# Decode attention with a token mixer: blocks of 16384 keys instead of 8192, 64 KB rows for V, and a new order of the loads at both ends

## The chip, the core and the metric

The kernel runs on one core of one Trainium2 chip. The metric is the device time of one execution in microseconds; the profile adds one execution taken by the hardware profiler.

## What is computed

One token `x` of 448 numbers goes through two branches, and a gate mixes them (bf16 inputs; the caches hold 65536 keys for each of 8 key heads, two query heads share one key head):

```python
g = sigmoid((x * gate_w).sum())                       # one number
q = (x @ wq).reshape(16 heads, 256)                   # wq: 448 x 4096
scores = q . k_cache * 256 ** -0.5                    # k_cache: 8 x 65536 x 256
o = softmax(scores) @ v_cache                         # v_cache: 8 x 65536 x 256
a = o.reshape(4096) @ wo                              # wo: 4096 x 448
h = layernorm(x)
b = gelu(outer(h, w1) + b1) @ w2 + b2                 # the mixer, 448 x 1792
out = g * a + (1 - g) * b
```

The two caches are 537 MB in all, read once.

## The kernel before

The work goes through 64 blocks of `BLK` = 8192 keys, eight for each key head. A block's K and V are each one load of 4 MB, in which a partition gets 64 consecutive keys, a row of 32 KB. There are two tiles for K and two for V, used in turn (`k_tiles`, `v_tiles`, 32 KB per partition each).

Every instruction that is recorded through `seq` is held to its order in the program on its own engine, so the order below is the order on each queue. All large loads stand on one queue, that of SyncE (SP). A load waits there until its tile is free, and whatever stands behind it on SP waits too. Besides, each load takes one of eight completion semaphores in turn, and waits until the load that held it before has landed.

Opening. SP loads `wq` (L109, three rows of 8 KB together on each partition, and the last 64 rows of the matrix in two loads, L112) into what is later a V tile. The queue of ScalarE (ACT) loads `x` three ways: copied to all partitions (`xb`, L115), as columns (`xm`, L117) and its last 64 numbers twice (`xt`, L119); then the mixer's small vectors and `gate_w` (L122 to L126). SP goes on with block 0's K in four pieces and block 1's K (L144, L145, issued at L132). TensorE forms the query with 128 matmuls (L194, L201), VectorE (DVE) the layernorm (L223 to L240), ScalarE fourteen gelu rows (`gel`, L245) into the other V tile. DVE then copies the query into `qpad` and computes `gate` (L267) from an exponential that stands on ScalarE behind the gelu rows (L256).

A block. `transposes` turns four groups of 128 keys on TensorE into a PSUM tile, one of three `tps`, and DVE copies it to `kT` (L316, L321). `scores` multiplies with the query (L331); it stands some groups behind the transposes. A block has 16 such groups of four. After the last scores of block `n` the program issues the load of V(n) and of K(n+2), takes the maximum of each row (L356), and does the product with V of the block before, `pv` (64 matmuls of 256 columns, L346), around the rest of the softmax. So `pv` runs one block behind the scores:

```python
        load_v(n, WHOLE if n < NBLK - 1 else LAST)
        if n + 2 < NBLK:
            load_k(n + 2, WHOLE)
        max_rows(n)
        if n > 0:
            pv(n - 1, 0, 32)
        max_heads(n)
        if n > 0:
            pv(n - 1, 32, KP)
        softmax(n)
```

In block 0 the load of `wo` (L462) and the mixer's product (`mixer_tail`, L280) stand between the scores and the load of V. When a key head is done, `denominators`, `head_out` and `project` carry its result through `wo` into `a_acc`, inside the next block's groups.

End. The V of the last block comes in five pieces (`LAST`: 2 MB, 1 MB, 512 KB and twice 256 KB). After the last piece come its `pv`, the accumulation (L400), `head_out` (L420), `project` (L433), two additions (L486, L487) and the store (L490).

Of the kernel before, what the change touches and what calls it, by code (L numbers as in the profile page):

```python
# [8 lines left out]
FP32 = mybir.dt.float32  # L9
# [10 lines left out]


BLK = 8192
KP = BLK // 128


NJ = 16
NI = KP // NJ
ROWS = REP * NI


@with_exitstack
def kernel(
# [26 lines left out]

    last = {}  # L60

    def seq(ins):
# [19 lines left out]
    v_tiles = [kvpool.tile([128, KP, DH], BF16, name=f"vt{i}") for i in range(2)]  # L82
    kT_tiles = [work.tile([128, NJ, 128, 2], BF16, name=f"kT{i}") for i in range(2)]
    p_tiles = [work.tile([128, 512], BF16, name=f"p_sb{i}") for i in range(2)]
    pT_tiles = [work.tile([128, 512], BF16, name=f"pT{i}") for i in range(2)]
    wo_sb = const.tile([128, HQ, 2, D], BF16)

    tps = [psum.tile([128, 512], FP32, name=f"tps{i}") for i in range(3)]
    sc_ps = [psum.tile([128, 512], FP32, name=f"sc_ps{i}") for i in range(2)]
    pv_ps = psum.tile([128, DH], FP32, name="pv_ps")  # L90
# [4 lines left out]
    xm = const.tile([128, 3], BF16)  # L95
    xt = const.tile([128, 1], BF16)
    xb = const.tile([128, D], BF16)
# [6 lines left out]
    wq_m = v_tiles[1][:, 0:48, :].rearrange("p a b -> p (a b)").rearrange(  # L104
        "p (k n) -> p k n", k=3
    )
    wq_t = v_tiles[1][:, 48:56, :].rearrange("p a b -> p (a b)")

    seq(nc.sync.dma_start(out=wq_m, in_=A_wq[0:DM, :].rearrange("(p k) n -> p k n", k=3)))  # L109
    DT = D - DM  # L110
    for h in range(2):
        seq(nc.sync.dma_start(  # L112
            out=wq_t[DT * h:DT * (h + 1), :], in_=A_wq[DM:D, 2048 * h:2048 * (h + 1)]
        ))
    seq(nc.scalar.dma_start(out=xb[:], in_=A_x[0, 0].partition_broadcast(128)))  # L115
    with nc.allow_non_contiguous_dma(reason="short rows"):
        seq(nc.scalar.dma_start(out=xm[:], in_=A_x[0, 0, 0:DM].rearrange("(p k) -> p k", k=3)))  # L117
        for h in range(2):
            seq(nc.scalar.dma_start(  # L119
                out=xt[DT * h:DT * (h + 1), :], in_=A_x[0, 0, DM:D].rearrange("(r o) -> r o", o=1)  # L120
            ))
        seq(nc.scalar.dma_start(out=w1b[:], in_=B_w1[0].rearrange("(p b) -> p b", b=NF)))  # L122
        seq(nc.scalar.dma_start(out=b1b[:], in_=B_b1.rearrange("(p b) -> p b", b=NF)))
        seq(nc.scalar.dma_start(out=w2b[:], in_=B_w2.rearrange("(p b) o -> p (b o)", b=NF)))
        seq(nc.scalar.dma_start(out=gw[:], in_=gate_w.rearrange("(o n) -> o n", o=1)))
        seq(nc.scalar.dma_start(out=b2b[:], in_=B_b2.rearrange("(o n) -> o n", o=1)))  # L126

    def load_k(n, pieces):
        g, b = divmod(n, NB)
        src = A_k_cache[0, g, b * BLK:(b + 1) * BLK, :].rearrange("(p j) d -> p j d", j=KP)  # L130
        for j0, j1 in pieces:
            seq(nc.sync.dma_start(out=k_tiles[n % 2][:, j0:j1, :], in_=src[:, j0:j1, :]))  # L132

    def load_v(n, pieces):
        g, b = divmod(n, NB)
        src = A_v_cache[0, g, b * BLK:(b + 1) * BLK, :].rearrange("(p j) d -> p j d", j=KP)
        for j0, j1 in pieces:
            seq(nc.sync.dma_start(out=v_tiles[n % 2][:, j0:j1, :], in_=src[:, j0:j1, :]))

    WHOLE = [(0, KP)]  # L140
    QUARTERS = [(i * NJ, (i + 1) * NJ) for i in range(NI)]
    LAST = [(0, 32), (32, 48), (48, 56), (56, 60), (60, 64)]

    load_k(0, QUARTERS)  # L144
    load_k(1, WHOLE)  # L145


# [4 lines left out]


    val = const.tile([128, REP], FP32)
    seq(nc.vector.tensor_reduce(
        out=val[:],
        in_=ident_f[:].rearrange("p (a i r) -> p r a i", a=4, r=REP)[:, :, :, 0:NI],
        op=ALU.add, axis=AXIS.XY,
    ))
    fst = const.tile([128, REP], FP32)  # L160
    seq(nc.vector.tensor_reduce(
        out=fst[:],
        in_=ident_f[:].rearrange("p (a i r) -> p r a i", a=4, r=REP)[:, :, :, 0:1],
        op=ALU.add, axis=AXIS.XY,
# [5 lines left out]
    ones_row = const.tile([1, 128], FP32)  # L170
    seq(nc.vector.memset(ones_row[:], 1.0))

# [9 lines left out]
    xtm = const.tile([128, 2], BF16)  # L182
    seq(nc.vector.memset(xtm[:], 0.0))
    for h in range(2):
        seq(nc.vector.tensor_copy(
            out=xtm[DT * h:DT * (h + 1), h:h + 1], in_=xt[DT * h:DT * (h + 1), :]
        ))
    q_ps = hd_ps[:, 0:2 * HQ]
    for h in range(HQ):
        half, hh = divmod(h, HQ // 2)  # L190
        for c in range(2):
            col = c * HQ + h
            for k in range(3):
                seq(nc.tensor.matmul(  # L194
                    q_ps[:, col:col + 1],
                    lhsT=wq_m[:, k, h * DH:(h + 1) * DH].rearrange("p (d c) -> p c d", c=2)[:, c, :],
                    rhs=xm[:, k:k + 1],
                    start=(k == 0),
                    stop=False,
                ))  # L200
            seq(nc.tensor.matmul(  # L201
                q_ps[:, col:col + 1],
                lhsT=wq_t[:, hh * DH:(hh + 1) * DH].rearrange("p (d c) -> p c d", c=2)[:, c, :],
                rhs=xtm[:, half:half + 1],
                start=False,
                stop=True,
            ))
# [12 lines left out]
    gel = v_tiles[0][:].rearrange("p a b -> p (a b)")[:, 0:NF * D].rearrange(  # L220
        "p (b n) -> p b n", b=NF
    )
    seq(nc.vector.tensor_copy(out=xf[:], in_=xb[:]))  # L223
# [25 lines left out]

# [8 lines left out]

    seq(nc.vector.tensor_copy(
# [14 lines left out]

# [18 lines left out]
    acc = work.tile([128, DH], FP32)  # L293
# [6 lines left out]
    den_tiles = [work.tile([128, 1], FP32, name=f"den{i}") for i in range(2)]  # L300
    al_tiles = [work.tile([128, 1], FP32, name=f"al{i}") for i in range(3)]
    rden = work.tile([128, 1], FP32)
    esc = work.tile([128, REP], FP32)
    oT = work.tile([128, 2, REP], BF16)
    a_acc = const.tile([1, D], FP32)
    res = const.tile([1, D], BF16)

    state = {"t": 0}

    def transposes(n, i, quarter):  # L310

        kT = kT_tiles[(n * NI + i) % 2]
        tp = tps[state["t"] % 3]
        state["t"] += 1
        for jj in range(4):
            seq(nc.tensor.transpose(  # L316
                tp[:, jj * 128:(jj + 1) * 128],
                k_tiles[n % 2][:, i * NJ + quarter * 4 + jj, :].bitcast(FP32),
                ident_f[:, :],
            ))  # L320
        seq(nc.vector.tensor_copy(  # L321
            out=kT[:, quarter * 4:(quarter + 1) * 4, :, :].rearrange("p j n c -> p (j n c)"),
# [3 lines left out]
    def scores(n, i, c):  # L326
        kT = kT_tiles[(n * NI + i) % 2]
        S = sc_ps[n % 2]
        g = n // NB
        for a in range(4):  # L330
            seq(nc.tensor.matmul(  # L331
                S[32 * a:32 * (a + 1), :],
                lhsT=qpad[:, c, g, i, :],
                rhs=kT[:, :, 32 * a:32 * (a + 1), c],
# [5 lines left out]
    def pv(n, j0, j1):  # L340
        pT = pT_tiles[n % 2]
        vt = v_tiles[n % 2]
        for j in range(j0, j1):
            i, jj = divmod(j, NJ)
            grp = j % 4
            seq(nc.tensor.matmul(  # L346
                pv_ps[32 * grp:32 * grp + REP, :],
                lhsT=pT[:, 32 * jj + REP * i:32 * jj + REP * (i + 1)],
                rhs=vt[:, j, :],
                start=(j < 4),  # L350
                stop=(j >= KP - 4),
# [3 lines left out]
    def max_rows(n):  # L355
        seq(nc.vector.tensor_reduce(  # L356
            out=rmax[:], in_=sc_ps[n % 2][:, :], op=ALU.max, axis=AXIS.X
        ))
        seq(nc.tensor.transpose(sm_ps[0:1, 0:128], rmax[:, 0:1], ident_f[:, :]))  # L359

    def max_heads(n):
        b = n % NB
# [5 lines left out]
        if b > 0:  # L368
            seq(nc.vector.tensor_tensor(out=mrun[:], in0=mrun[:], in1=mnew[:], op=ALU.max))
        seq(nc.tensor.matmul(  # L370
            sm_ps[:, 128:128 + REP], lhsT=ones_row[0:1, :], rhs=mrun[0:1, :], start=True, stop=True
        ))

    def softmax(n):
        b = n % NB
        nb, nb_old = nb_tiles[n % 2], nb_tiles[(n + 1) % 2]
        den, al = den_tiles[n % 2], al_tiles[n % 3]
        seq(nc.vector.tensor_tensor_reduce(  # L378
            out=junk[:], in0=sm_ps[:, 128:128 + REP], in1=nval[:], scale=1.0, scalar=0.0,
            op0=ALU.mult, op1=ALU.add, accum_out=nb[:, 0:1],  # L380
        ))
        if b > 0:
# [3 lines left out]
        seq(nc.scalar.activation(  # L386
            out=p_tiles[n % 2][:, :], in_=sc_ps[n % 2][:, :], func=ACT.Exp, scale=scale,
            bias=nb[:, 0:1], accum_out=den[:, 0:1],
        ))
        seq(nc.vector.transpose(out=pT_tiles[n % 2][:, :], in_=p_tiles[n % 2][:, :]))  # L390
# [7 lines left out]
    def accumulate(n):  # L398
        if n % NB > 0:
            seq(nc.vector.scalar_tensor_tensor(  # L400
                out=acc[:], in0=acc[:], scalar=al_tiles[n % 3][:, 0:1], in1=pv_ps[:, :],
                op0=ALU.mult, op1=ALU.add,
            ))
        else:
            seq(nc.vector.tensor_copy(out=acc[:], in_=pv_ps[:, :]))
# [11 lines left out]
    def head_out():  # L417

        for c in range(2):
            seq(nc.tensor.matmul(  # L420
                hd_ps[:, 464 + REP * c:464 + REP * (c + 1)],
                lhsT=acc[:].rearrange("p (d c) -> p c d", c=2)[:, c, :], rhs=esc[:],
                start=True, stop=True,
            ))
        seq(nc.vector.tensor_copy(
            out=oT[:], in_=hd_ps[:, 464:464 + 2 * REP].rearrange("p (c r) -> p c r", c=2)
        ))

    def project(g):
        a_ps = hd_ps[0:1, 0:D]  # L430
        for r in range(REP):
            for c in range(2):
# [3 lines left out]
                ))  # L436
        if g == 0:
# [83 lines left out]
```

## Time and profile before

| what | value |
|---|---|
| median of 3 runs | 1296.43 us (1296.35 to 1297.05) |
| the profiled execution's own time | 1297.59 us |
| its span, first to last instruction | 1295.8 us |
| busy share: TensorE matmul, weight load, VectorE, ScalarE | 76%, 54%, 64%, 6% |
| mean granted TensorE clock | 0.904 |
| read from HBM | 544.34 MB, 420 GB/s over the span |
| loads of 4 MB: K, V | 63, 63; 27.3 and 32.2 us from issue to landing (median) |

The profile gives busy time in microseconds for each engine, a rate and a share for the 16 DMA engines, and for each group of instructions its count, its mean duration and what ended the idle time before it. A share over the whole span is a mean over stages; the stages here are the opening (about 50 us), the blocks, and the end (about 30 us). A load's time from issue to landing includes the time it is queued behind other loads.

### The profile page before, as it was taken

How to read it: one execution, taken by the hardware profiler on the slowest of the kernel's cores; microseconds unless marked ns; L12 is line 12 of the kernel's file. 1: busy time of each engine (PE TensorE's matmuls, PEld its weight loads, DVE VectorE, ACT ScalarE, POOL GpSimd, SP SyncE). 2: the span in 40 equal slices, each digit the busy share in tenths (PEclk: the TensorE clock that was granted, in tenths of full speed). 3: DMA queues.
4: the chain of work that ended last, by engine and by line, in shares of the span. 5: the costliest groups of instructions: out<-in, count | busy, mean ns of one | idle time of the engine just before them, and what ended most of it. 6: DMA issues, size and time to landing. Idle time of an engine off the chain costs nothing.

```text
span 1295.8 us, 24075 instructions
## 1 busy us (share of the span) xinstructions
PE 983.7 (76%) x10654; PEld 705.8 (54%) x10654; DVE 823.9 (64%) x1599; ACT 73.5 (6%) x203; POOL 2.4 (0%) x7
## 2 busy tenths in 40 slices
PE   3877877877877877778878778778778687777786
PEld 2554655555654655555655555546556456555554
DVE  3665766756766666666657657567566566666664
ACT  4000000000000000000000000000000000000000
POOL 0000000000000000000000000000000000000000
PEclk9988989988989889889889889898898898889898
DMA  8999999999999999999999999999999999999995
GB/s 333 412 430 429 432 430 426 434 426 432 431 426 432 429 430 431 427 433 432 427 432 429 430 430 429 432 426 432 432 424 434 427 430 432 426 421 425 429 429 218
DMA packets 22798, 545.88 MB, mean 421 GB/s; under 512 B 2980, under 2 KB 5158, under 8 KB 5670
## 3 DMA queue, kind: packets, MB, share of 16 engines
q1 hardware_dynamic: 21810, 544.22, 98.2%
q8 instruction: 83, 1.36, 0.4%
q10 hardware_dynamic: 884, 0.13, 0.1%
q14 instruction: 21, 0.17, 0.0%
HBM read 544.34 MB, written 0.00 MB: 420 GB/s over the span
## 4 chain that ended last, share of the span: by engine, by line
DMA 66%; PE 31%; DVE 1%; ACT 1%; issue 0%; ACTq 0%; SPq 0%; DVEq 0%
DMA kn<-in_A_k_cache_dram 64%; PE tps L316 24%; PE sc_ps L331 5%; DMA vt<-in_A_v_cache_dram 2%; DMA xt<-in_A_x_dram 1%; ACT vt L245 1%; PE hd_ps L433 1%; PE pv_ps L346 0%; PE hd_ps L420 0%; DVE kT L321 0%; PE hd_ps L280 0%; DVE rmax L356 0%; ACT L256 0%; PE sm_ps L370 0%; PE sm_ps L359 0%
## 5 line engine op out<-in xcount | busy, mean ns | idle before, releaser
L321 DVE COPY kT<-tps 128x1024 bf16<-128x1024 bf16 x1024 | 655.6, 685 | 231.8 <-PE tps L316 229.3
L316 PE MATMUL tps<-ident_f,kn 128*128 128x128 f32 x4096 | 642.2, 309 | 177.3 <-DMA kn<-in_A_k_cache_dram 172.2
L316 PEld LDWEIGHTS tps<-ident_f,kn 128*128 128x128 f32 x4096 | 522.9, 158 | 294.3 <-DMA kn<-in_A_k_cache_dram 189.7
L331 PE MATMUL sc_ps<-kT,qpad 128*32 128x512 bf16 x2048 | 195.4, 392 | 50.0 <-DVE kT L321 49.2
L346 PE MATMUL pv_ps<-vt,pT 128*2 128x256 bf16 x4096 | 148.4, 291 | 1.3 <-DMA vt<-in_A_v_cache_dram 1.2
L331 PEld LDWEIGHTS <-qpad 128*32 128x32 bf16 x2048 | 52.9, 93 | 126.8 <-issue 117.2
L346 PEld LDWEIGHTS <-pT 128*2 128x2 bf16 x4096 | 90.1, 87 | 28.0 <-issue 2.4
L390 DVE STREAM_TRANSPOSE pT<-p_sb 128x512 bf16<-128x512 bf16 x64 | 45.5, 711 | 64.8 <-ACT p_sb L386 64.8
L383 ACT ACTIVATE al<-nb,nb 128x1 f32<-128x1 f32 x56 | 16.5, 295 | 1038.5 <-DVE nb L378 1038.5
L356 DVE TENSOR_REDUCE rmax<-sc_ps 128x1 f32<-128x512 f32 x64 | 44.2, 691 | 45.5 <-PE sc_ps L331 45.5
L359 PE MATMUL sm_ps<-ident_f,rmax 128*1 128x128 f32 x64 | 17.3, 270 | 52.4 <-DVE rmax L356 52.4
L378 DVE CUSTOM_DVE_ANT_0 junk<-sm_ps,nval 128x2 f32<-128x2 f32 x64 | 10.2, 159 | 68.9 <-PE sm_ps L370 68.9
L386 ACT ACTIVATE p_sb<-sc_ps,nb 128x512 bf16<-128x512 f32 x64 | 42.9, 670 | 156.7 <-DVE nb L378 156.7
L359 PEld LDWEIGHTS sm_ps<-ident_f,rmax 128*1 128x1 f32 x64 | 5.1, 79 | 84.4 <-DVE rmax L356 84.4
L370 PEld LDWEIGHTS sm_ps<-mrun,ones_row 1*128 1x128 f32 x128 | 20.8, 202 | 16.7 <-issue 16.2
L400 DVE SCALAR_TENSOR_TENSOR acc<-acc,al,pv_ps 128x256 f32<-128x256 f32 x56 | 26.5, 472 | 4.0 <-PE pv_ps L346 4.0
L370 PE MATMUL sm_ps<-mrun,ones_row 1*128 1x2 f32 x128 | 26.3, 272 | 0.3 <-DVE mrun L363 0.3
L363 DVE TENSOR_REDUCE mnew<-sm_ps 1x2 f32<-1x32 f32 x56 | 10.0, 178 | 20.3 <-PE sm_ps L359 20.3
L194 PE MATMUL hd_ps<-xm,vt 128*128 128x1 bf16 x96 | 3.6, 165 | 12.4 <-DMA xm<-in_A_x_dram 12.4
L386 ACT ACTIVATION_READ_ACCUMULATOR p_sb<-sc_ps,nb 128x1 f32 x64 | 12.2, 191 | 0.0
L194 PEld LDWEIGHTS <-vt 128*128 128x128 bf16 x96 | 3.6, 104 | 12.3 <-DMA vt<-in_A_wq_dram 12.1
L392 DVE SCALAR_TENSOR_TENSOR lsum<-lsum,al,den 128x1 f32<-128x1 f32 x56 | 9.9, 177 | 0.0
(66 smaller groups left out, 94.2 us busy)
## 6 DMA issues: line engine op xcount, KB each, us to landing
kn<-in_A_k_cache_dram SPq DMA_DIRECT2D x63, 4096.0 KB, 27.3
vt<-in_A_v_cache_dram SPq DMA_DIRECT2D x63, 4096.0 KB, 32.2
kn<-in_A_k_cache_dram SPq DMA_DIRECT2D x4, 1024.0 KB, 11.1
wo_sb<-in_A_wo_dram SPq DMA_DIRECT2D x1, 3584.0 KB
vt<-in_A_wq_dram SPq DMA_DIRECT2D x1, 3072.0 KB
vt<-in_A_v_cache_dram SPq DMA_DIRECT2D x1, 2048.0 KB, 19.7
vt<-in_A_v_cache_dram SPq DMA_DIRECT2D x1, 1024.0 KB
vt<-in_A_wq_dram SPq DMA_DIRECT2D x2, 256.0 KB, 4.1
```

The lines of the kernel that those rows point to most:

```text
L245: seq(nc.scalar.activation(out=gel[:, b, :], in_=h_bc[:], func=ACT.Gelu_apprx_tanh, scale=w1f[:, b:b + 1], bias=b1f[:, b:b + 1],))
L316: seq(nc.tensor.transpose(tp[:, jj * 128:(jj + 1) * 128], k_tiles[n % 2][:, i * NJ + quarter * 4 + jj, :].bitcast(FP32), ident_f[:, :],))
L321: seq(nc.vector.tensor_copy(out=kT[:, quarter * 4:(quarter + 1) * 4, :, :].rearrange("p j n c -> p (j n c)"), in_=tp[:, :].bitcast(BF16),))
L331: seq(nc.tensor.matmul(S[32 * a:32 * (a + 1), :], lhsT=qpad[:, c, g, i, :], rhs=kT[:, :, 32 * a:32 * (a + 1), c], start=(i == 0 and c == 0 ...
L346: seq(nc.tensor.matmul(pv_ps[32 * grp:32 * grp + REP, :], lhsT=pT[:, 32 * jj + REP * i:32 * jj + REP * (i + 1)], rhs=vt[:, j, :], start=(j ...
L356: seq(nc.vector.tensor_reduce(out=rmax[:], in_=sc_ps[n % 2][:, :], op=ALU.max, axis=AXIS.X))
L359: seq(nc.tensor.transpose(sm_ps[0:1, 0:128], rmax[:, 0:1], ident_f[:, :]))
L370: seq(nc.tensor.matmul(sm_ps[:, 128:128 + REP], lhsT=ones_row[0:1, :], rhs=mrun[0:1, :], start=True, stop=True))
L383: seq(nc.scalar.activation(out=al[:], in_=nb_old[:], func=ACT.Exp, scale=-1.0, bias=nb[:, 0:1]))
L386: seq(nc.scalar.activation(out=p_tiles[n % 2][:, :], in_=sc_ps[n % 2][:, :], func=ACT.Exp, scale=scale, bias=nb[:, 0:1], accum_out=den[:, ...
L390: seq(nc.vector.transpose(out=pT_tiles[n % 2][:, :], in_=p_tiles[n % 2][:, :]))
L400: seq(nc.vector.scalar_tensor_tensor(out=acc[:], in0=acc[:], scalar=al_tiles[n % 3][:, 0:1], in1=pv_ps[:, :], op0=ALU.mult, op1=ALU.add,))
```

## The change

A block now has 16384 keys, so there are 32 blocks, four for each key head. On a partition a block has 128 consecutive keys, 64 KB in each cache.

- V has one tile, `vt`, of 64 KB per partition, and one load of 8 MB per block. K keeps two tiles; they are the two halves of one block, each a load of 4 MB with 32 KB from every 64 KB row.
- `pv_block` does a block's product with V behind its own softmax. A matmul takes two keys' rows at once, 512 columns (64 matmuls for 16384 keys instead of 128), and the even and odd parts are added when a head ends (`collect`).
- There are four `tps` tiles and one `sc_ps`. A block has 32 groups of four transposes, `NI` = 8 query columns instead of 4.
- `x` comes as one row of 896 bytes, first on ACT's queue. Five small matmuls spread it over the partitions. The last 64 rows of `wq` are one load.
- `wq` and `gel` lie in `vt`. The mixer's product stands in block 0 behind the twelfth group; the load of V(0) follows the scores, and the load of `wo` follows that of V(0).
- For the last but one block, K of the last block is loaded ahead of V. The last block's V goes into the two K tiles, in six pieces.
- At the end, the last two keys of each pair are multiplied directly into the head's output behind `collect`, and `1/denominator` and the gate's other part are worked out ahead of it (`rdv`, `base`).

The diff, cut to its core:

```diff
-BLK = 8192
-KP = BLK // 128
+BLK = 16384
+VP = BLK // 128
+KP = VP // 2
 NJ = 16
-NI = KP // NJ
+NI = VP // NJ
+TAIL = 2
...
-    v_tiles = [kvpool.tile([128, KP, DH], BF16, name=f"vt{i}") for i in range(2)]
+    vt = kvpool.tile([128, VP, DH], BF16, name="vt")
...
-    tps = [psum.tile([128, 512], FP32, name=f"tps{i}") for i in range(3)]
-    sc_ps = [psum.tile([128, 512], FP32, name=f"sc_ps{i}") for i in range(2)]
-    pv_ps = psum.tile([128, DH], FP32, name="pv_ps")
+    tps = [psum.tile([128, 512], FP32, name=f"tps{i}") for i in range(4)]
+    sc_ps = psum.tile([128, 512], FP32, name="sc_ps")
+    pv_ps = psum.tile([128, 2, DH], FP32, name="pv_ps")
...
+    def rows(cache, n):
+        g, b = divmod(n, NB)
+        return cache[0, g, b * BLK:(b + 1) * BLK, :].rearrange("(p j) d -> p j d", j=VP)
+
+    def load_k(n, h, pieces=((0, KP),)):
+        for j0, j1 in pieces:
+            seq(nc.sync.dma_start(
+                out=k_tiles[h][:, j0:j1, :],
+                in_=rows(A_k_cache, n)[:, h * KP + j0:h * KP + j1, :],
+            ))
+
+    def load_v(n):
+        seq(nc.sync.dma_start(out=vt[:, :, :], in_=rows(A_v_cache, n)))
...
+    def load_v_last(n):
+        src = rows(A_v_cache, n)
+        seq(nc.sync.dma_start(out=k_tiles[0][:, :, :], in_=src[:, 0:KP, :]))
+        seq(nc.sync.dma_start(out=k_tiles[1][:, 0:32, :], in_=src[:, KP:KP + 32, :]))
+        for j0, j1 in ((0, 8), (8, 12), (12, NJ - TAIL), (NJ - TAIL, NJ)):
+            seq(nc.sync.dma_start(
+                out=pairs(k_tiles[1][:, 32:64, :])[:, :, j0:j1, :],
+                in_=pairs(src[:, KP + 32:VP, :])[:, :, j0:j1, :],
+            ))
+
+    seq(nc.scalar.dma_start(out=xr[:], in_=A_x[0, 0].rearrange("(o n) -> o n", o=1)))
     seq(nc.sync.dma_start(out=wq_m, in_=A_wq[0:DM, :].rearrange("(p k) n -> p k n", k=3)))
-    DT = D - DM
-    for h in range(2):
-        seq(nc.sync.dma_start(
-            out=wq_t[DT * h:DT * (h + 1), :], in_=A_wq[DM:D, 2048 * h:2048 * (h + 1)]
-        ))
-    seq(nc.scalar.dma_start(out=xb[:], in_=A_x[0, 0].partition_broadcast(128)))
+    seq(nc.sync.dma_start(
+        out=wq_t[:, :], in_=A_wq[DM:D, :].rearrange("r (h n) -> (r h) n", h=2)
+    ))
...
-    load_k(0, QUARTERS)
-    load_k(1, WHOLE)
+    load_k(0, 0, ((0, 32), (32, KP)))
+    load_k(0, 1)
...
+    x_col = hd_ps[:, 40:44]
+    for k in range(3):
+        seq(nc.tensor.matmul(
+            x_col[:, k:k + 1], lhsT=xr[:, 0:DM].rearrange("o (p k) -> o k p", k=3)[:, k, :],
+            rhs=ones_b[:, 0:1], start=True, stop=True,
+        ))
...
+            if between is not None and t == 11:
+                between()
...
+    def pv(ip, j0, j1, v, first, final, end=NJ):
+        for jj in range(j0, j1):
+            grp = jj % 4
+            seq(nc.tensor.matmul(
+                pv_ps[32 * grp:32 * grp + 2 * REP, :, :],
+                lhsT=pT[:, 32 * jj + 2 * REP * ip:32 * jj + 2 * REP * (ip + 1)],
+                rhs=pairs(v)[:, :, jj, :],
...
+    L = NBLK - 1
+    for n in range(NBLK):
+        score_block(n, mixer_tail if n == 0 else None)
+        if n < L:
+            if n == L - 1:
+                load_k(L, 0)
+                load_k(L, 1)
+                load_v(n)
+            else:
+                load_v(n)
+                if n == 0:
+                    seq(nc.sync.dma_start(
+                        out=wo_sb[:], in_=A_wo.rearrange("(h r2 par) n -> r2 h par n", r2=128, par=2)
+                    ))
+                load_k(n + 1, 0)
+                load_k(n + 1, 1)
+        if n == L:
+            load_v_last(L)
+            pv_block()
+            accumulate(n - 1)
...
+        softmax(n)
+        if n < L - 1:
+            if n % NB == NB - 1:
+                denominators()
+            pv_block()
+            accumulate(n)
+            if n % NB == NB - 1:
+                head_end(n // NB)
...
+    pv(3, 12, NJ - TAIL, v_end, False, True, NJ - TAIL)
+    accumulate(L)
+    collect(fst, False)
+    for jj in range(NJ - TAIL, NJ):
+        for e in range(2):
+            for c in range(2):
+                seq(nc.tensor.matmul(
+                    o_ps[c],
+                    lhsT=pairs(v_end)[:, e, jj, :].rearrange("p (d c) -> p c d", c=2)[:, c, :],
+                    rhs=pT[:, 32 * jj + 2 * REP * 3 + REP * e:32 * jj + 2 * REP * 3 + REP * (e + 1)],
+                    start=False, stop=(jj == NJ - 1 and e == 1),
+                ))
+    for c in range(2):
+        seq(nc.vector.tensor_tensor(out=oT[:, c, :], in0=o_ps[c], in1=rdv[:], op=ALU.mult))
     project(HKV - 1)
```

## The prediction

> **What bounds the kernel now.** I read the page first (span, slices), then busy time by stretch, then the timeline of both ends. The mean rate hides the ends, so the slices come first.
>
> ```profile
> span 1295.8 us, 24075 instructions
> DMA  8999999999999999999999999999999999999995
> GB/s 333 412 430 429 432 430 426 434 426 432 431 426 432 429 430 431 427 433 432 427 432 429 430 430 429 432 426 432 432 424 434 427 430 432 426 421 425 429 429 218
> q8 instruction: 83, 1.36, 0.4%
> ```
>
> DMA is full in every slice but the first and the last; no other engine passes 76%. Stretches (columns: PE, PEld, DVE, ACT, POOL busy with counts, PE clock, DMA share, GB/s):
>
> ```profile
> 2.00:10.00 8.00, 0.00 (x0) 0.00 (x0) 1.15 (x8) 0.00 (x0) 0.97 (x2) 1.00 0.90 346
> 10.00:14.00 4.00, 0.22 (x3) 0.23 (x3) 1.23 (x4) 0.95 (x1) 0.00 (x0) 1.00 0.35 86
> 14.00:20.00 6.00, 2.33 (x88) 2.36 (x89) 3.66 (x17) 4.76 (x8) 0.00 (x0) 1.00 0.97 322
> 100.00:1100.00 1000.00, 772.24 (x8352) 556.10 (x8352) 646.58 (x1239) 47.91 (x147) 0.00 (x0) 0.90 1.00 430
> 1276.00:1284.00 8.00, 5.30 (x95) 3.04 (x93) 4.71 (x13) 0.96 (x3) 0.00 (x0) 1.00 0.55 230
> 1288.40:1295.80 7.40, 3.05 (x12) 1.35 (x11) 1.92 (x4) 0.00 (x0) 0.00 (x0) 0.50 0.00 0
> ```
>
> Three things can be won: a hole at 10 to 20 us, the middle at 430 GB/s, an end of 20 us. At 1276:1284 the share is 0.55: only nine of 16 DMA engines still work. The trace's landings show why. At the start the 16 engines finish a load within 1 us of each other; at the end seven are 10 to 12.7 us ahead. The lag grows in steps of about 1.1 us, one for each of the 83 instruction-fetch packets (16 KB, 1.07 us), which fall on the other nine. So the end is set by the slowest engine, and what the fast ones wait costs nothing.
>
> The opening (start us, us, engine, line) and the waits of the load queue (total us, times, longest):
>
> ```profile
> 0.73 0.41 SPq L109 DMA_DIRECT2D vt<-in_A_wq_dram  x1
> 12.41 1.18 SPq L112 DMA_DIRECT2D vt<-in_A_wq_dram  x2
> 13.64 3.52 SPq L132 DMA_DIRECT2D kn<-in_A_k_cache_dram  x5
> 27.83 0.14 DVE L267 TENSOR_SCALAR gate<-ez 1x1 f32<-1x1 f32 x1 [6.07 <-ACT ez L256]
> 40.89 2.81 PE L280 MATMUL hd_ps<-vt,w2b 128*1 128x448 bf16 x14
> 43.73 0.34 SPq L138 DMA_DIRECT2D vt<-in_A_v_cache_dram  x1
> SPq L138 <- PE hd_ps L280: 26.0, 1, 26.0
> ```
>
> SP stands from 1.1 to 12.4 us because a load takes one of eight completion semaphores in turn and waits for its last holder, here the small x loads. The first V waits for the mixer's 14 matmuls (L280), those for the block's transposes, and these for DVE, which waits at `gate` (L267) for ACT.
>
> **The change, part by part.** Sums are on the profiled execution (span 1295.8, own time 1297.59, so 1.8 lies outside the span); the median of the runs, 1296.43, is 1.2 below it, and I add the difference to the median.
>
> *Opening, a gain.* One 896-byte x row replaces four small x loads, and the wq tail becomes one load, so eight DMAs stand ahead of K instead of twelve, and none waits for a semaphore. By the built order K's first piece now waits for the x row alone. A single-row load landed 0.7 us after its issue on an idle queue (out, at the end), and the packet records show the ACT queue's packets served one for one with wq's 24 KB packets (0.93 us), so x lands by about 4 us, and K is queued before wq ends (11.8). The hole closes: 4 x (1 - 86/434) = 3.2 and 6 x (1 - 322/434) = 1.5, together **-4.7** (3.2 to 5.5). Block 0's K then ends at 32.9 instead of 37.6.
>
> *Opening, a loss.* Before, wo (L462, 3.6 MB, 9.5 us in the landings) was queued ahead of the first V and kept the stream fed until 47.05, after V's issue at 43.73. Now wo stands behind V on SP, V is one tile that holds wq and the gelu rows, and the built order makes its load wait for the 14th mixer matmul. When is that? b1b landed at 13.1 (issue 3.68 + 9.4). It lands no earlier after: w1b's eight packets per engine alternate with wq's eight, b1b's with those of the wq tail. From b1f to h_bc 2.5, gelus 9.23, table load and exp 1.5, gate 0.35: DVE reaches the first kT copy at 26.8 (before 28.1). TensorE's x spread is five small matmuls at 4 us, under that wait, at nothing; were it exposed, five rows like L194's 0.17 us. Twelve groups took 8.7 us after the gate (28.16 to about 36.85); with a fourth `tps` buffer 8.3; mixer 2.8: issue at 38.0. Issue to first packet took 0.96 (1263.54 to 1264.50): 39.0. The stream has been dry since 32.9: **+6.1** (3.5 to 8). Together +1.4: V starts at 39.0 with wo's 9.5 still to come, against 47.05 with it done.
>
> *Middle.* Loads stay queued ahead. With T the landing of V(n-1): `pv_block` (64 matmuls of 512 columns; 32 of 256 took 1.04, so about 4.2 warm, 6 cold) frees `vt` at T+6, and V(n) is needed at T+19.5. K's first half is free at T+21, needed at T+39; the second at T+32, needed at T+48.7. Slack of 13 us or more covers softmax, which now stands bare before `pv_block` (about 4 us of PE idle): nothing. If that cover were gone it would be 4 us a block, 120 in all. Each block's cost is its bytes.
>
> *Rows of 64 KB.* Packets of 32 KB took 1215 ns, 16 KB 613, 8 KB 312: a line with 11 ns per packet. V has 31 x 8 rows of 64 KB on each engine: 248 x 11 ns = **-2.7** if a row is one packet, 0 if it is cut in two. No row shows a 64 KB packet; I take the first, as 8, 16, 24 and 32 KB rows all went as one.
>
> The Trainium skill (DMA: Bandwidth & Descriptors, Anatomy of one DMA) gives about 2.0 us fixed per DMA, measured on the gpsimd path; an estimate by it would be 32 fewer V loads x 2 = -64. The row against it is 430 GB/s over 1000 us: the cost is hidden behind queued loads.
>
> *Pitch.* K's rows are now 32 KB pieces at a 64 KB pitch instead of adjacent. Before, pieces of 2 to 16 KB at a 32 KB pitch ran on the same line as whole rows, so I take 0; 64 KB is not shown (0 to +6, half a per cent of 1230).
>
> The same page (Latency and other measured facts) speaks against the change: copies at a 512 KiB pitch ran at 207 GB/s and a padded pitch at 214; an estimate by that 3% would be +40 us. It has no 64 KB row, nor does this trace.
>
> *Fewer instructions.* `pv` halves to 2048 matmuls, each with a weight load; PE drops from 21308 to about 17100 instructions, 67 fetches of 256 instead of 83. The slowest engine's lag falls from 12.7 by a fifth, -2.4; since idle stretches line the engines up anew, I take **-1.9** (-2.6 to -1.2).
>
> *Last loads swapped.* K(31) is queued before V(30), so it follows K(30) directly, and needs K(30)'s buffers. A block half took 10.5 to 12.9 us from first transpose to release, median 11.7:
>
> ```profile
> 47.04 4.50 PE L316 MATMUL tps<-ident_f,kn 128*128 128x128 f32 x24
> 58.82 0.33 SPq L132 DMA_DIRECT2D kn<-in_A_k_cache_dram  x1
> ```
>
> With V(29) landed at 0, K(30) lands at 9.75 and 19.5. The first half is free at 9.75 + 11.3, the new load's data flow at 22.1: a hole of 2.6. The second half is free 10.84 later (2.71 per four groups, DVE-bound), data at 33.0; K(31)'s first half ended at 31.9: 1.1. V(30) cannot fill either, it stands behind on SP. **+3.7** (2.0 to 5.3). V(31) then reuses the K tiles in time (free at 47 and 58, wanted at 62 and 72): nothing.
>
> *Last pieces.* 8.4 MB of V(31) in its six pieces: 9.72 + 4.9 + 2.55 + 1.35 + 0.78 + 0.78 = 20.1 us; the last 8.4 MB before took 19.7: **+0.4**.
>
> *Tail.* Before, 7.4 us after the last landing (1288.36). Gone: L486 (0.61) and acc's place behind the last piece. But the piece of rows 12 and 13 lands only 0.8 earlier, and behind it stand pv 0.65, acc on 512 columns (472 ns for 256, so 0.75), eight fp32 passes of `collect` (four took 1.01 at clock 0.50, so 2.0), eight small matmuls 1.0: matmuls end 3.6 after the last landing, where before they ended 2.06 after. With one more DVE step (0.2) and L486 gone: **+1.1** (-0.5 to +1.5).
>
> Sum: -4.7 + 6.1 - 2.7 - 1.9 + 3.7 + 0.4 + 1.1 = +2.0, so 1296.43 + 2.0 = 1298.4.
>
> **The rivals.**
> *Rows cut in two (slower).* If a 64 KB row goes as two 32 KB packets, the -2.7 is gone: +4.7, 1301.1. For it: nothing above 32 KB is shown. Against: every row so far was one packet. It decides as soon as 0.6 of the 2.7 is missing.
> *The holes do not open (faster).* If b1 lands early, or transposes run faster than before, V's issue comes by 33.5 and the first hole is 1.6; releases at 10.5 make the others 2.0; a warm tail +0.5. Sum -4.7 + 1.6 - 2.7 - 1.9 + 2.0 + 0.4 + 0.5 = -4.8: 1291.6. Against: the one-for-one packets. It decides from 4.6 us less hole than I count.
> *The pitch costs (slower).* One per cent on 1230 us is +12.3: 1310.7. Only the unshown pitch speaks for it.
>
> **How the numbers follow.** Forecast 0.52, rows cut 0.20, holes closed 0.17, pitch 0.08, other 0.03. Where 0.2% (2.6 us) is about what a measurement of this kernel can tell from no change, the forecast at +2.0 lies inside it in about two thirds of its cases and above it in the rest; rows cut nine in ten slower; holes closed three in four faster. That gives faster 0.16, same 0.40, slower 0.44. The forecast's own range is 1295.5 to 1301; with rows cut, and most of the faster rival, 1293.0 to 1302.8.
>
> **What would show it.** Right: no hole at 10 to 20 us, a dry stretch near 33 to 39, V packets of 65536 bytes near 2.42 us, about 67 fetches, two short holes some 62 and 50 us before the last landing, about 8.5 us behind it. Wrong: V issued before 34; a middle away from 430 GB/s by over 1%; any hole that repeats with the block (then the single `vt` is late).

## The result: 1304.4 us, 0.6% slower

The changed kernel takes 1304.40 us (median of 5 runs, 1300.96 to 1305.01), the kernel before 1296.35 (1295.17 to 1297.05): a ratio of 1.0058, 95% interval 1.0043 to 1.0072. The prediction was 1298.4, at most 1302.8. The profiled execution took 1304.43 us, with a span of 1302.6; its counterpart has 1295.8.

Page of the changed kernel: span, busy share of the DMA engines in 40 slices, GB/s in the same slices, instruction fetches.

```profile
span 1302.6 us, 19720 instructions
DMA  8799999999999999999999999999999999999697
GB/s 371 323 435 445 415 430 430 440 436 424 425 432 432 438 431 434 417 432 434 435 437 425 430 427 433 432 443 422 431 427 431 429 422 437 425 428 430 273 420 291
q8 instruction: 67, 1.10, 0.3%
```

Two slices stand out that were full before: the second (323) and the third from the end (273). The busy times by stretch (columns as in the prediction's table) place the losses:

```profile
10.00:14.00 4.00, 1.79 (x61) 1.72 (x62) 0.32 (x3) 0.59 (x1) 0.00 (x0) 1.00 1.07 441
14.00:20.00 6.00, 4.52 (x85) 4.43 (x83) 2.32 (x12) 3.77 (x6) 0.00 (x0) 1.00 1.01 421
32.00:40.00 8.00, 8.00 (x59) 4.98 (x56) 4.81 (x10) 0.00 (x0) 0.00 (x0) 1.00 0.31 101
40.00:43.00 3.00, 2.46 (x24) 1.84 (x23) 3.00 (x6) 0.00 (x0) 0.00 (x0) 1.00 0.83 350
100.00:1100.00 1000.00, 777.22 (x6666) 500.66 (x6662) 589.20 (x1038) 23.86 (x72) 0.00 (x0) 0.84 1.00 431
1219.00:1226.00 7.00, 7.00 (x42) 6.01 (x42) 4.84 (x7) 0.00 (x0) 0.00 (x0) 0.63 0.47 201
1226.00:1233.00 7.00, 7.00 (x65) 5.02 (x63) 6.47 (x11) 0.00 (x0) 0.00 (x0) 1.00 0.25 75
```

The old hole at 10 to 20 us is closed (86 and 322 GB/s before, 441 and 421 now), the middle runs at 431. In exchange the stream is nearly dry at 32 to 40 us and at 1219 to 1233 us. In both stretches TensorE is busy throughout: the loads wait for compute. The timeline names the two waits (start us, us, engine, line, count, and the idle time ahead with what ended it; SPq is the load queue):

```profile
35.76 2.81 PE L291 MATMUL hd_ps<-vt,w2b 128*1 128x448 bf16 x14
38.60 0.33 SPq L116 DMA_DIRECT2D vt<-in_A_v_cache_dram  x1
38.97 0.43 SPq L477 DMA_DIRECT2D wo_sb<-in_A_wo_dram  x1
1218.79 5.38 PE L327 MATMUL tps<-ident_f,kn 128*128 128x128 f32 x24 [3.67 <-DMA kn<-in_A_k_cache_dram]
1231.49 11.16 SPq L110 DMA_DIRECT2D kn<-in_A_k_cache_dram  x2
```

V(0) is issued behind the mixer's matmuls, and wo 0.4 us behind V(0). K(31) is issued 12.7 us after the landing of K(30)'s first half (1218.75), when that half has been transposed.

A table makes the account exact. Every kernel here moves the same caches and the same wo, so I compare four stretches by the landing on the slowest DMA engine (each load marks its end once on each of the 16 engines; the last mark counts): the opening (two loads' worth of K, wo and 8 MB more, 20.4 MB in all), the next 116 units of 4 MB (to V(29)'s landing), the last 33.6 MB, and what lies behind the last landing. In us:

| kernel | opening | middle | last 33.6 MB | tail | span |
|---|---|---|---|---|---|
| before | 68.16 | 1140.7 | 79.5 | 7.4 | 1295.8 |
| changed | 71.24 | 1137.8 | 86.9 | 6.7 | 1302.6 |
| difference | +3.1 | -2.9 | +7.4 | -0.8 | +6.8 |
| as predicted | +1.4 | -4.6 | +4.1 | +1.1 | +2.0 |

(The medians differ by 8.0, not 6.8, because the profiled execution of before was 1.2 us above its median.)

### The profile page after: what moved, and what is told of

It reads as the page before. It is cut to its first block, busy times and chain, and to the rows that moved or that the text cites. A ratio compares the mean times of both kernels' runs of the same rounds, so it can differ in the third digit from the quotient of the medians.

```text
span 1302.6 us, 19720 instructions
## 1 busy us (share of the span) xinstructions
PE 993.0 (76%) x8553; PEld 642.7 (49%) x8553; DVE 755.6 (58%) x1358; ACT 42.7 (3%) x107; POOL 4.2 (0%) x7
## 4 chain that ended last, share of the span: by engine, by line
DMA 67%; PE 30%; DVE 2%; ACT 1%; issue 0%; ACTq 0%
DMA kn<-in_A_k_cache_dram 64%; PE tps L327 24%; PE sc_ps L341 6%; DMA kn<-in_A_v_cache_dram 2%; DVE kT L332 1%; DMA b1b<-in_B_b_dram 1%; ACT vt L238 1%; PE hd_ps L291 0%; PE hd_ps L450 0%; ACT L248 0%; PE hd_ps L439 0%; PE sm_ps L439 0%; DVE acc L417 0%; DVE rmax L383 0%; DVE y_sb L295 0%
## 5 line engine op out<-in xcount | busy, mean ns | idle before, releaser
L327 PE MATMUL tps<-ident_f,kn 128*128 128x128 f32 x4096 | 610.6, 299 | 113.9 <-DMA kn<-in_A_k_cache_dram 107.0
L327 PEld LDWEIGHTS tps<-ident_f,kn 128*128 128x128 f32 x4096 | 493.0, 152 | 236.4 <-DMA kn<-in_A_k_cache_dram 124.1
L367 PE MATMUL pv_ps<-vt,pT 128*4 128x512 bf16 x1984 | 179.1, 540 | 89.7 <-DMA vt<-in_A_v_cache_dram 82.1
L367 PEld LDWEIGHTS <-pT 128*4 128x4 bf16 x2046 | 61.8, 111 | 202.6 <-issue 144.1
L417 DVE SCALAR_TENSOR_TENSOR acc<-acc,al,pv_ps 128x512 f32<-128x512 f32 x24 | 17.9, 748 | 170.9 <-PE pv_ps L367 170.9
L399 ACT ACTIVATE p_sb<-sc_ps,nb 128x512 bf16<-128x512 f32 x32 | 22.0, 687 | 1228.8 <-DVE nb L395 1228.8
L407 DVE STREAM_TRANSPOSE pT<-p_sb 128x512 bf16<-128x512 bf16 x32 | 22.8, 711 | 28.9 <-ACT p_sb L399 28.9
L383 DVE TENSOR_REDUCE rmax<-sc_ps 128x1 f32<-128x512 f32 x32 | 22.1, 691 | 22.8 <-PE sc_ps L341 22.8
L392 PE MATMUL sm_ps<-mrun,ones_f 1*128 1x2 f32 x64 | 15.2, 304 | 14.2 <-DVE mrun L391 11.7
L392 PEld LDWEIGHTS sm_ps<-mrun,ones_f 1*128 1x128 f32 x64 | 12.4, 240 | 20.3 <-DVE mrun L391 16.3
```

The lines of the kernel that those rows point to most:

```text
L327: seq(nc.tensor.transpose(tp[:, jj * 128:(jj + 1) * 128], k_tiles[i // 4][:, i % 4 * NJ + quarter * 4 + jj, :].bitcast(FP32), ident_f[:, :],))
L367: seq(nc.tensor.matmul(pv_ps[32 * grp:32 * grp + 2 * REP, :, :], lhsT=pT[:, 32 * jj + 2 * REP * ip:32 * jj + 2 * REP * (ip + 1)], rhs=pair ...
L383: seq(nc.vector.tensor_reduce(out=rmax[:], in_=sc_ps[:, :], op=ALU.max, axis=AXIS.X))
L392: seq(nc.tensor.matmul(sm_ps[:, 128:128 + REP], lhsT=ones_f[0:1, :], rhs=mrun[0:1, :], start=True, stop=True))
L399: seq(nc.scalar.activation(out=p_sb[:, :], in_=sc_ps[:, :], func=ACT.Exp, scale=scale, bias=nb[:, 0:1], accum_out=den[:, 0:1],))
L407: seq(nc.vector.transpose(out=pT[:, :], in_=p_sb[:, :]))
```

## The experiments

Theory A: the loss comes from the two stretches in which the load queue runs dry, and the way to each is a load that waits for compute. Theory B: the steady stream itself became slower (rows, pitch, the single V tile). Theory C: only the end matters. Each run's time is compared with the changed kernel's 1304.40, its ratio with the kernel before. Line numbers are those of each kernel's own file.

### wo ahead of V(0)

```diff
     load_k(0, 1)
+    seq(nc.sync.dma_start(out=wo_sb[:], in_=A_wo.rearrange(...)))
...
-                if n == 0:
-                    seq(nc.sync.dma_start(out=wo_sb[:], ...))
```

> wo is loaded right behind block 0's K instead of behind V(0). Theory A (the 8 us over the kernel before come from two stretches in which the load queue runs dry, and from the slow start of the stream behind each): wo fills the stretch from 32.0 to 39.6 us, V(0) lands at 61.0 to 62.5 us instead of wo at 71.24, so the time falls by 8 to 10 us, to 1294 to 1297, a ratio of 0.998 to 1.001 to the kernel before. Theory B (the steady stream is slower: rows of 64 KB, the 64 KB pitch or the single V tile): the opening is not the cause and at most 2 us are won, 1302 or more. Theory C (the end is the cause, the opening's dry stretch is hidden by later slack): less than 2 us too, with V(0) at 62 all the same.

Measured: 1294.83 us, ratio 0.9986 (0.9977 to 0.9995), 9.6 us under the changed kernel. Windows of this kernel:

```profile
32.00:40.00 8.00, 8.00 (x62) 4.61 (x60) 5.48 (x11) 0.00 (x0) 0.00 (x0) 1.00 1.05 380
```

380 GB/s instead of 101: wo fills the stretch while V(0) waits. V(0) landed at 62.11 where the changed kernel had both at 71.24, so the opening's loss is 9.1 us. The place of one load decided more than the whole difference between the kernels. B and C fall.

### The mixer earlier in block 0

```diff
-            if between is not None and t == 11:
+            if between is not None and t == 2:
```

> The mixer's 14 matmuls stand behind the third group of block 0 instead of the twelfth; nothing else differs from the changed kernel, wo stays behind V(0). Theory A: the gelu rows are done at about 26.5 us, the matmuls at 29.4, V(0) is issued at about 29.5 instead of 38.6, before K ends at 32.0, so the opening has no dry stretch: 1294 to 1296.5 as with wo first. Rival (V(0) is held by the scores of block 0 rather than by the mixer, or wo itself was what was won): V(0) issued after 36, at most 3 us won, 1301 or more.

Measured: 1294.99 us, ratio 0.9987 (0.9978 to 0.9996). Timeline of this kernel:

```profile
26.41 0.33 SPq L116 DMA_DIRECT2D vt<-in_A_v_cache_dram  x1
26.78 0.43 SPq L477 DMA_DIRECT2D wo_sb<-in_A_wo_dram  x1
```

The issue was 3 us earlier still than expected, because the matmuls follow the gelu rows one by one (5.24 us from 21.13). V(0) and wo had landed at 61.99. The loads stand in the changed kernel's order, so it is the wait that costs, not the order.

### The kernel before with the new opening alone

Only `x` as one row, spread by TensorE, and the wq tail in one load were put into the kernel before.

> The kernel before with one part of the change alone: x as one row spread by TensorE, and the wq tail in one load. The prediction's first term by itself: the hole at 10 to 20 us closes and everything behind it moves by 4.4 to 4.7 us, 1291.5 to 1292.5, a ratio of 0.996 to 0.997. If the kernel before hides the opening's hole later (it is the lag of the slowest DMA engine that counts at the end): under 1.5 us, 1295 or more.

Measured: 1293.58 us, ratio 0.9979 (0.997 to 0.9988): 2.6 us, between the two expectations. Timeline of this kernel:

```profile
39.57 2.81 PE L296 MATMUL hd_ps<-vt,w2b 128*1 128x448 bf16 x14
42.41 0.34 SPq L129 DMA_DIRECT2D vt<-in_A_v_cache_dram  x1
```

Block 0's and block 1's K landed 4.7 us earlier on the slowest engine (33.49 against 38.16), but V(0)'s issue moved only from 43.73 to 42.41, and wo's landing moved up to meet it: the stream carried 257 and 279 GB/s at 42 to 46 us, and the opening ended at 65.62, 2.5 us earlier. The rest of the gain waits for the mixer, as the next run shows.

### The same, with the mixer behind the third group

```diff
+            if n == 0 and t == 2:
+                mixer_tail()
...
-            mixer_tail()
         load_v(n, WHOLE if n < NBLK - 1 else LAST)
```

> The kernel before with the new loads of x and wq's tail, and the mixer's 14 matmuls behind the third group of block 0. With the new loads alone V(0)'s issue moved only from 43.73 to 42.41 us and the landing of block 1's V moved by 2.5 us, though K landed 4.1 to 4.7 us earlier. If the mixer's place is what keeps the rest: V(0) issued before 36, no gap behind wo, the landings 4 to 4.7 us earlier than in the kernel before, 1291.5 to 1292.3. If it is anything else: as with the new loads alone, 1293 or more.

Measured: 1290.47 us, ratio 0.9957 (0.9944 to 0.9969). V(0) was issued at 25.08, the opening ended at 62.05, 6.1 us earlier than before, and the time fell by 5.8. That is a microsecond under the range expected. The opening's part of the change, done without a wait, is worth 6 us on the old blocks. That is 1.3 us more than the hole counted in the prediction; 1.0 of it lies in wo's load, whose slowest engine took 10.6 us in the kernel before (38.16 to 48.73) and 9.6 here (33.05 to 42.63).

### V in rows of 32 KB

```diff
-        seq(nc.sync.dma_start(out=vt[:, :, :], in_=rows(A_v_cache, n)))
+        for h in range(2):
+            seq(nc.sync.dma_start(out=vt[:, h * KP:(h + 1) * KP, :], in_=rows(A_v_cache, n)[:, h * KP:(h + 1) * KP, :]))
```

> V(0) to V(30) are loaded as two loads of 4 MB each, rows of 32 KB at a pitch of 64 KB, as K is; all else as in the changed kernel. If a packet costs 11 ns of its own (248 more packets on each DMA engine), the middle gets 2.7 us longer, 1306 to 1308 on the median. If rows of 64 KB cost something (theory B), it gets faster, by 3 us or more. If the pitch of 64 KB cost something, V now shows it as K does, and it gets slower by far more than 3 us.

Measured: 1306.41 us, ratio 1.0075 (1.0063 to 1.0088), 2.0 us above the changed kernel. V(29) landed 1.8 us later (1210.89 against 1209.06), but this run's opening had ended 0.8 us earlier (70.40): its middle took 1140.5 us, 2.7 more than the changed kernel's. The packet records give a little less: from one packet's start to the next it is 1212 ns for 32 KB and 2417 for 64 KB (medians), 7 ns less than two halves, 1.7 us in 240 rows. So 64 KB rows gain 1.7 to 2.7 us, not lose. With K and V both at the 64 KB pitch, this kernel's window still shows the rate of before:

```profile
100.00:1100.00 1000.00, 771.83 (x6667) 503.50 (x6666) 590.86 (x1039) 23.89 (x72) 0.00 (x0) 0.86 1.00 430
```

The pitch costs nothing here: with 32 KB rows the middle took 1140.5 us at the 64 KB pitch and 1140.7 with adjacent rows, in the kernel before. The run also bounds the price of a load: 31 more of them, and twice the packets for V, cost 2.0 us in all, under 0.1 us each.

The Trainium skill (DMA: Bandwidth & Descriptors, Anatomy of one DMA) gives about 2.0 us fixed per DMA on the gpsimd path; an estimate by it is 62 us for 31 loads. For these loads, queued on SyncE, the 2.0 us measured for all of them decide.

### The usual order at the end

```diff
-            if n == L - 1:
-                load_k(L, 0)
-                load_k(L, 1)
-                load_v(n)
-            else:
-                load_v(n)
+            load_v(n)
...
-        seq(nc.sync.dma_start(out=k_tiles[0][:, :, :], in_=src[:, 0:KP, :]))
+        seq(nc.sync.dma_start(out=vt[:, 0:KP, :], in_=src[:, 0:KP, :]))
```

(and so on for the other pieces; block 30's `pv_block` follows its own softmax.)

> At the end the usual order is kept: V(30) ahead of K(31), block 30's product in its usual place, and the last V goes into the V tile in the same six pieces. Theory A: no load waits for a buffer that is still being scored, so from V(29)'s landing to the last landing it takes 80 to 82 us instead of 86.9; the time falls by 4 to 6.5 us, to 1298 to 1300, and the rest of the loss (the opening) stays. Theory B: at most 1 us. Theory C: all of the loss to the kernel before goes, 8 us or more.

Measured: 1301.41 us, ratio 1.0039 (1.0026 to 1.0052): 3.0 us won, less than expected, though the last 33.6 MB took 79.0 us instead of 86.9. The stream won 7.9 us and the tail gave back 5.3 (12.0 us behind the last landing instead of 6.7). The next run has the same end, and shows why.

### Both: wo first and the usual order

> wo first and the usual order at the end, together. Theory A: both gains add, 13 to 16 us: 1288 to 1291, a ratio of 0.993 to 0.996 to the kernel before, and the time no longer follows the granted TensorE clock from run to run (spread under 1.5 us, where the changed kernel's five runs spread over 4). Theory B: 1301 or more.

Measured: 1292.25 us, ratio 0.9971 (0.9959 to 0.9982): 12.2 us won, not 13 to 16, and the six runs spread over 1.8 us, not under 1.5. The last landing came at 1279.42, the end 11.8 us later. Timeline of this kernel:

```profile
1249.88 5.38 PE L330 MATMUL tps<-ident_f,kn 128*128 128x128 f32 x24 [3.36 <-DMA kn<-in_A_k_cache_dram]
1275.10 0.69 DVE L386 TENSOR_REDUCE rmax<-sc_ps 128x1 f32<-128x512 f32 x1
1279.95 5.25 PE L370 MATMUL pv_ps<-vt,pT 128*4 128x512 bf16 x62
```

From K(31)'s landing (1249.84) scoring takes 25 us, the softmax 5, the product 5.3, the rest 6: 41.4 us, and that chain ends last. The swap had bought something: K(31) early enough for this chain. The end has two limits, and the two orders each meet one.

### V(30) in two halves, K(31) between them

```diff
-                load_k(L, 0)
-                load_k(L, 1)
-                load_v(n)
+                for h in range(2):
+                    seq(nc.sync.dma_start(out=vt[:, h * KP:(h + 1) * KP, :], in_=rows(A_v_cache, n)[:, h * KP:(h + 1) * KP, :]))
+                    if h == 0:
+                        load_k(L, 0)
+                        load_k(L, 1)
```

wo is first here too.

> wo first, and at the end V(30) in two halves of 4 MB with K(31) between them; the last V goes into the K tiles as in the changed kernel. Theory A1 (the end has two limits: with K(31) right behind K(30) the queue runs dry, 7.8 us, and with K(31) behind all of V(30) the chain from its landing, 41.3 us of scores, softmax, product and tail, ends last): the half of V(30) lasts 9.75 us, which covers the wait for the first K tile, and K(31) still lands 9.7 us earlier than in the usual order. No dry stretch near the end, at most 7.5 us behind the last landing, 1287 to 1289, 4 us under the run with both changes. Rival (the chain of block 30 and block 31 on TensorE and VectorE is the limit in any order): over 10 us behind the last landing again, 1291 to 1293.

Measured: 1289.07 us (1287.04 to 1289.71), ratio 0.994 (0.9927 to 0.9952). The last 33.6 MB took 79.2 us, so the queue was never dry for the slowest engine. The end came 8.2 us behind the last landing (1279.75), not 7.5 as expected. The windows look otherwise:

```profile
1219.00:1226.00 7.00, 7.00 (x65) 5.02 (x63) 6.33 (x11) 0.00 (x0) 0.00 (x0) 1.00 0.73 290
```

At 290 GB/s some engines wait for K(31)'s issue at 1223.00; but the landings of V(30)'s first half were 12 us apart by then (1217.73 to 1229.70). It is the engines ahead that wait, and that costs nothing.

### Block 30's product earlier

```diff
-            if between is not None and t == 11:
+            if between is not None and t == (11 if n == 0 else 27):
...
+        if n == L - 1:
+            pv_block(0, 2)
```

(`between` in block 31 is the product's second half and its accumulation.)

> The run with V(30) split, and block 30's product moved: its first half right behind softmax(30), where TensorE idled 3.1 us, its second half and the accumulation behind the 28th group of block 31. In the run with V(30) split, the last product (62 matmuls, 6.37 us from 1274.94) ended 1.6 us behind the last landing of 1279.75. Theory A1: that chain is now 3 to 4 us earlier, the landing is the limit again, 6.7 us from the last landing to the end of the span, 1287 to 1288. Rival (the inserted matmuls push block 31's own scores back by as much): 1289 or more.

Measured: 1288.79 us (1288.61 to 1289.17), ratio 0.9943 (0.9931 to 0.9956), 7.2 us from the last landing (1279.79) to the end. Block 31's product starts 2.7 us earlier (1272.21) and waits for the last pieces again, but the median moved by only 0.3 us against the run above, and the two intervals overlap. The time does not refute the rival, and 1287 to 1288 was missed. It is the fastest version of all runs here: 7.5 us under the kernel before in the same runs (1296.24), 15.6 under the changed one.

### Keeping TensorE busy ahead of block 30

The changed kernel with added matmuls from `wo_sb` into free PSUM ahead of `score_block(30)`.

```diff
+        if n == L - 1:
+            for _ in range(48):    # second run: 16
+                seq(nc.tensor.matmul(hd_ps[0:32, 0:D], lhsT=qpad[:, 0, 0, 0, :], rhs=wo_sb[:, 0, 0, :], start=True, stop=True))
```

> The changed kernel with 48 added matmuls (448 columns, from wo into a free corner of PSUM, read by nobody) ahead of block 30's transposes, where TensorE idles 3.7 us until K(30)'s first half lands. If the idle time is what halves the granted clock at 1217.4 to 1224.2, and the halved clock is what lengthens the dry stretch: the first 24 transposes take about 3 us instead of 5.38, K(31) is issued 2 to 2.5 us earlier than 12.7 us behind K(30)'s landing, and the time falls by 2 to 2.5 us, to 1301.5 to 1302.5. If VectorE's copies or the landing set the release, or the clock falls for another reason: within 0.5 us of the changed kernel, or slower where the added matmuls themselves are late.

Measured: 1308.15 us, ratio 1.0089 (1.0075 to 1.0103). The size was wrong: 48 matmuls took 9.24 us, 193 ns each, and put off the transposes to 1224.41. From there all went as expected of a full clock (24 transposes in 2.84 us, K(31) issued 10.6 us later), but 5.6 us late. With 16 of them:

> As the run with 48 added matmuls, which took 9.24 us instead of the 3.7 us wanted, with 16 of them (3.1 us at 193 ns each, from 1215.2 to 1218.3), so that they end before K(30)'s first half lands at 1218.8. If idle time halves the granted clock, and the halved clock lengthens the dry stretch: the first 24 transposes take 2.84 us, K(31) is issued 10.6 us behind the landing instead of 12.7, and the time falls by about 2 us, to 1302 to 1303. If the clock falls all the same, or something else sets the release: within 0.7 us of the changed kernel.

Measured: 1301.94 us (1300.99 to 1302.39), ratio 1.0044 (1.003 to 1.0057), 2.5 us under the changed kernel. Timeline of the run with 16:

```profile
1214.34 3.19 PE L470 MATMUL hd_ps<-wo_sb,qpad 128*32 128x448 bf16 x16
1218.27 2.84 PE L327 MATMUL tps<-ident_f,kn 128*128 128x128 f32 x24 [0.74 <-DMA kn<-in_A_k_cache_dram]
1228.85 11.15 SPq L110 DMA_DIRECT2D kn<-in_A_k_cache_dram  x2
```

24 transposes took 2.84 us instead of 5.38, K(31) was issued 10.6 us behind the landing (1218.23) instead of 12.7, and the last 33.6 MB took 84.4 us instead of 86.9. Two microseconds of the hole at the end were the halved clock. The landings carry this more than the medians do, since the changed kernel's five runs spread over 4 us; among these the time falls as the mean granted clock rises (1305.01 us at 0.840, 1300.96 at 0.871), which fits but is a correlation. The windows of the two kernels at the same place, the changed one first:

```profile
1217.40:1224.20 6.80, 5.41 (x28) 5.08 (x28) 3.46 (x5) 0.00 (x0) 0.00 (x0) 0.50 0.50 217
```

```profile
1217.40:1224.20 6.80, 5.66 (x49) 4.52 (x48) 5.03 (x9) 0.00 (x0) 0.00 (x0) 1.00 0.53 226
```

The Trainium skill (TensorE: Matmul & The Clock Gate, Part 1) says that an idle window of about 3.4 us halves the clock and a busy one restores it. The runs agree: 3.7 us of idle time, a clock of 0.50; filled, 1.00.

## Why the prediction was wrong, step by step

The mechanism of the two holes was the right one, and none of the three rivals decided. V went in packets of 65536 bytes (median 2.42 us), not cut in two; the pitch cost nothing; the holes did open. V(0) was issued at 38.60 where 38.0 was forecast. The step that failed is the price of the two holes: the sum put them at the time the queue stands dry, 6.1 and 3.7 us, and they cost 9.1 and about 7. Three more terms were off, one of them with the other sign.

- **Opening, a loss: +6.1 forecast, 9.1 measured** (71.24 against 62.11 with wo first). The dry stretch on the slowest engine had the forecast size: K ended at 33.43, V(0)'s first packet came at 39.55, 6.1 us. Left out was what follows. The first 16 packets took 2.50 to 3.44 us instead of 2.42, the window at 40 to 43 us shows 350 GB/s, and V(0) landed 20.9 us behind its first packet instead of 19.4: 1.5 us. Then wo's slowest engine took 10.8 us instead of 9.5: 1.3 us.
- **Opening, a gain: -4.7 forecast.** It is 6.1 with the stream kept full (68.16 to 62.05 or 62.11), but alone on the kernel before only 2.5, as long as V(0) waits for a late mixer. The prediction added a gain and a loss as if each were worth its sum by itself; the two are one wait. It also put the end of wo in the kernel before at 47.05; on the slowest engine it is 48.73.
- **Last loads swapped: +3.7 forecast, about 7 measured.** K(31)'s first half landed 15.0 us behind K(30)'s second half on fifteen engines (16.4 on the last one) instead of 9.7, its second half 11.3 behind that: 5.3 and 1.6 us, for 2.6 and 1.1. Release took 12.7 us instead of the 11.3 taken. The rows gave 10.5 to 12.9, and the sum took less than their median of 11.7. The cause of the upper end stands in the profile of before, where 24 transposes at a granted clock of 0.50 take 5.38 us and the next load of K is issued 12.75 us after their start, against 3.29 and 10.6 at a clock of 1.00 (rows of the chain that ended last: start us, us):

```profile
1110.21 3.29 PE tps L316 x24
1120.79 29.94 DMA kn<-in_A_k_cache_dram
1208.91 5.38 PE tps L316 x24
1221.66 26.05 DMA kn<-in_A_k_cache_dram
```

In this place the prediction's own numbers held the idle time: `pv_block` ends 4 to 6 us behind V(29)'s landing, K(30) lands 9.75 behind it. The rest is again a slow start: 281 GB/s at 1242 to 1246 us. The last pieces were sized well: with both limits avoided, the last 33.6 MB take 79.2 us, 79.5 before.
- **Middle: -4.6 forecast, -2.9 measured.** Here the term for fewer instructions failed more than the one for the rows. The rows are worth 1.7 to 2.7 us, for 2.7 (the run with 32 KB rows). That leaves 0.2 to 1.2 for the instructions instead of 1.9. Compared directly, with 32 KB rows in both, 83 fetches go with a middle of 1140.7 us (before; 1140.6 and 1140.7 in the two runs with its new opening) and 67 with 1140.5. The lag of the slowest engine at V(29), from which the term was taken, does not follow the fetches: 12.93 us before, 11.97 after, and 13.69 in the run with 32 KB rows, which has 67 fetches too. Why so little of it reaches the time is open. The middle had nothing repeating with the block, as forecast.
- **Tail: +1.1 forecast, -0.8 measured.** The price list was too dear in two places. The small matmuls of the last two rows took 0.35 us together, not 1.0, and `collect` started at 1295.92, with the last landing at 1295.95 and not behind it:

```profile
1295.12 0.75 DVE L417 SCALAR_TENSOR_TENSOR acc<-acc,al,pv_ps 128x512 f32<-128x512 f32 x1 [8.28 <-PE pv_ps L367]
1295.92 1.01 PE L439 MATMUL hd_ps<-fst,acc 128*128 128x2 f32 x4 [0.84 <-DVE acc L417]
1298.22 1.65 PE L450 MATMUL hd_ps<-wo_sb,oT 128*1 128x448 bf16 x4 [0.23 <-DVE oT L526]
```

The gap of 4.8 us in the sum is 1.7 (opening) + 1.7 (middle) + 3.3 (end) - 1.9 (tail): the tail's error hid part of the others. The other 1.2 us between 1298.4 and 1304.4 are the difference between before's profiled execution and its median. The range failed because each hole was bounded by its dry time alone. A hole's lower bound is the dry time; the price of the restart should have stood above it.

Open remains why the first packets after a dry stretch are slow. The tails of kernels with the same end differ by up to 1.2 us (7.4 in the kernel before, 6.2 with its new opening), and nearly all of that goes with the granted clock behind the last landing, 0.50 against 0.79: four fp32 matmuls of `head_out` took 1.01 us against 0.63, those of `project` 1.65 against 0.92.

## What to carry to other kernels

Where the loads are the limit, ask of each large load what compute it waits for, and put loads that wait for nothing (here wo) ahead of it: the place of one 3.7 MB load was worth 9.6 us, the larger blocks about 3 in the middle. The old blocks with the new opening and the earlier mixer come within 1.7 us of the best version with larger ones (1290.47 against 1288.79). At the end two limits pull against each other, the buffer that must be freed and the chain behind the last input, and half a load between them can satisfy both. Price a dry stretch with its restart and with compute at the clock it will have after idling, not at the median.

## What the runs showed of the hardware

- A stretch without loads costs more than its length: 16 packets of 64 KB at 2.50 to 3.44 us instead of 2.42, and 8 MB landing 1.5 us later than at that pace.
- 3.7 us without matmuls halved the granted clock for 6.8 us, and with 16 otherwise useless matmuls in that gap it stayed at 1.00 and the last 33.6 MB took 84.4 us instead of 86.9.
- 448-column matmuls into one set of 32 PSUM partitions took 193 ns each at full clock, while 64 matmuls of 512 columns spread over four such sets took 3.63 us in the run with V(30) split, 57 ns each.
- A low mean rate can be free: with 290 GB/s for 7 us, where it was the engines ahead that waited, the last 33.6 MB took 79.2 us, and 79.5 in the kernel before.
